# Weights converted in pairs of blocks, q and k in one transfer, and a new planned order in a fused attention and gated-MLP kernel

## The chip, the cores and the metric

The kernel runs on one core of a Trainium2 chip. The metric is the device time of one execution in microseconds (us), less is better. TensorE (PE) does matrix products into PSUM, VectorE (DVE), ScalarE (ACT) and GpSimd (POOL) work on data in SBUF (and, but for POOL, in PSUM), and all transfers are issued by SyncE (SP).

## The reference

Two steps follow each other, in float32, with a batch of 8, 576 positions, 8 heads of 64, a model width of 512 and an inner width of 1,024. The weights come as float64.

```python
scores = scale * np.matmul(q, k.transpose(0, 1, 3, 2))
mask_local = (rel >= 0) & (rel < 32)                          # heads 0..3
mask_strided = (rel >= 0) & (pos[None, :] % 32 == pos[:, None] % 32)   # heads 4..7
attn = softmax(np.where(masks, scores, -1e9))
x = (attn @ v).transpose(0, 2, 1, 3).reshape(B, S, H * D)

h = np.maximum(x @ w_in, 0.0)
conv_out = sum over k of conv_w[k] * h shifted by k - 1 along the positions
gate = 1.0 / (1.0 + np.exp(-conv_out))
out = (h * gate) @ w_out
```

## The kernel before

**Attention** is done by head pairs: four for each batch, 32 in all, in the order 0, 2, 1, 3. Positions of the strided heads are permuted on the host, so that both masks become a band of 64 keys for each block of 32 queries. For one head pair `probabilities` (lines 422 to 463) puts mask and scores in one half of the PSUM bank group `r` (lines 433, 442), takes the maximum (454), subtracts it (455), takes the exponential on ACT (457), sums (458), inverts (460), scales on POOL (461) and transposes on DVE (463). `values` (465 to 521) multiplies with v (482) into both halves of `r`, and then stores the result x as a sum of two operands of the fast matmul format: the high part `xh` is a cast on ACT (518), the low part `xl` is the difference on DVE (519). The scores of the next head pair stand ahead of the values of this one. There are two sets of buffers for q, k and v.

**The weights** arrive as float64 words. For one block of 512 elements a partition, `from_f64` (329 to 343) builds a float32 and a tail from the two words: an absolute value on ACT (333) and five instructions on DVE (334, 336, 338, 340, 342), through the work tiles `wa` and `wt`. `convert` (359 to 396) then makes a high and a low part of the weight, in one of three ways that a letter of `SPLIT_W` picks for each of the sixteen blocks: `a` makes the low part on PE with three products (385, 386, 388) and a cast on ACT (389); `v` does less on PE (392, 393) and adds on DVE (395); `p` and `q` add on POOL (376). Eight blocks hold w_in and eight w_out. Three of the first blocks land in the tile `misc`, which later holds h; the others in two tiles `ws`.

**The MLP** runs over nine groups of 512 positions. `mm1` (541 to 560) is the first layer: for each f of eight, four chunks of the model width, three products each (high by high, low weight by high, high weight by low, line 553). `conv_gate` (562 to 595) does ReLU on ACT (569), carries two columns to the next group on POOL (571, 573), multiplies by the middle tap (579 or 582), adds the other two on DVE (588), takes the sigmoid (591) and the gate product (593), and splits the result into `gh` (405) and `gl` (408). `mm2` (597 to 624) is the second layer, again three products for each f (612), a copy from PSUM (618) and the transfer out (622, 624). `gh` and `gl` have rows of 514 words for each f. PSUM has four banks `m` for both layers and for the conversions.

**The order** of all instructions on all engines comes from a planner (class `Plan`, 61 to 242). Every `op` gives an engine, an estimated duration, a due time `at`, and what it reads and writes; `order` (87 to 164) walks a model of the engines in time and, on each, takes the ready operation with the least due time. The due times are made from the constants at lines 26 to 58. `FIRST` orders the first transfers and conversions. The model of the transfers has the constants `RATE` (a rate), `AHEAD` (how far transfers are issued ahead) and two at lines 148 and 149. While PE waits in the first batch, a few products of zeros (`WARM`, `WARM_SCORES`, `WARM_VALUES`; lines 449 and 491) are put in.

Of the kernel before, what the change touches and what calls it, by code (L numbers as in the profile page):

```python
# [10 lines left out]
F32 = _mybir.dt.float32  # L11
# [10 lines left out]
W = 32  # L22
# [5 lines left out]
AHEAD = 4.0  # L28
ACT_PENALTY = 0
PE_PENALTY = 1  # L30
RATE = 212.0
SWITCH = 0.1

EYE_AT = -56.45
MASK_AT = [-7061.8, -67.27]
CONV_AT = 1385.62
# [4 lines left out]
FIRST_AT = [10013.72, -673.01, -2108.52, 354.38, -675.63]  # L41
CG = [-4502.12, -3977.93, -595.29, 279.54, 48.45, 1488.79, -926.05, -8.92]
AT = [-81.82, -823.34, 1719.98, 17.64, 1599.9, -3890.54, 1345.53, -249.03, 373.38, -2039.0]
GROUP_AT = [330.52, 57.25, -611.52, -158.19, -150.04, -174.24, 1340.78, 429.88, 10027.77]
MM1_STEP = 184.14
MM2_AT = [2846.14, 3562.43, 4063.58, 1041.1, -789.0, 1030.2, 1543.77, -2620.09, 3072.12]
MM2_STEP = 3698.29
ATTENTION_AT = [[1642.69, -1181.42, 70.28, 1735.09], [-58.27, 1008.41, -184.07, -40618.96], [2456.96, 1326.28, -665.66, 1109.36], [-769.08, -2427.12, 1428.65, 831.45], [467.77, 1376.9, 1.5, 781.18], [-13410.3, 547.67, 1062.12, -6885.62], [-5118.76, 1131.26, -697.05, 294.98]]
LOAD_Q = -4714.94
LOAD_V = -1312.32  # L50
W_IN_AT = [1388.4, -1343.86, -1012.12, -1705.32, -1354.59, 160.36, 671.61, -934.52]
W_OUT_AT = [3058.3, -555.74, -1216.5, -322.67, 371.26, -447.54, -1462.81, -8211.41]
SPLIT_W = "vaqaavaavvvaavaa"
SPLIT_G = "vvvvvvvv"
FIRST_SPLIT_G = "vvvvvpvp"
MAJOR = 0
FIRST_GATE = "vvpppppv"
FIRST_SCALE = "aaaaaaaa"


class Plan:
# [25 lines left out]
    def order(self, at):  # L87
# [17 lines left out]
        while True:  # L105
# [41 lines left out]
            if e == "dma":  # L147
                moved = max(moved, t + 1.3) + dur * 1024 / RATE / 1000
                free[e] = max(t + 0.6, moved - AHEAD)
# [96 lines left out]
def tile_banded_attention_gated_mlp(ctx, tc, qT, kT, vw, w_in, conv, w_out, masks_in, picks_in, eye_in, out):  # L246
    nc = tc.nc
    B, NHP, _, S = qT.shape
# [16 lines left out]
    def attention_buffers(pool, i):  # L265
        return (pool.tile([P, S], F32, name=f"q{i}"), pool.tile([P, SP], F32, name=f"k{i}"),
# [17 lines left out]
    gh = mlp.tile([P, NF, N + 2], F32R, name="gh")  # L284
    gl = mlp.tile([P, NF, N + 2], F32R, name="gl")
# [11 lines left out]
    NWS, NWA, NWT, NWL = 2, 2, 2, 2  # L297
# [11 lines left out]
    def load_q(n, at):  # L309
        i, b, hp = slot(n), n // NHP, HPS[n % NHP]  # L310
        q = buffers[i][0]
        op(Q, 288, at, lambda: nc.sync.dma_start(out=q, in_=qT[b, hp]), (), [("q", i)])

    def load_k(n, at):
        i, b, hp = slot(n), n // NHP, HPS[n % NHP]
        k = buffers[i][1]
        op(Q, 288, at, lambda: nc.sync.dma_start(out=k[:, W:], in_=kT[b, hp]), (), [("k", i)])
# [6 lines left out]
    def set_up(i):  # L324
        k, t = buffers[i][1], buffers[i][3]
        op(G, 0.12, -10, lambda: nc.gpsimd.memset(k[:, :W], 0.0), (), [("kpad", i)])
        op(G, 0.11, -3, lambda: nc.gpsimd.memset(t[:, :, 64:65], 1e-9), (), [("tcol", i)])

    def from_f64(hi, lo, a, t, tail, at, kw, ka, kt, kl, short):
        n = 0.15 if short else 0.418  # L330
        m = 0.15 if short else 0.69
        af = a.bitcast(F32)
        op(A, 0.2 if short else 0.667, at, lambda: nc.scalar.activation(out=af, in_=hi.bitcast(F32), func=AF.Abs), [kw], [ka])
# [5 lines left out]
                                                            op1=ALU.bitwise_or), [kw, ka], [kt], lock=True)  # L339
        op(V, n, at, lambda: nc.vector.tensor_scalar(out=a, in0=t, scalar1=-0x800000, scalar2=None,  # L340
                                                     op0=ALU.bitwise_and), [kt], [ka], lock=True)
        op(V, m, at, lambda: nc.vector.scalar_tensor_tensor(out=tail, in0=lo.bitcast(U32), scalar=2.0 ** -52, in1=af,
                                                            op0=ALU.mult, op1=ALU.mult), [kw, ka], [kl], lock=True)

    def convert_conv(at):
# [3 lines left out]
        from_f64(cwords[:, :, 1], cwords[:, :, 0], cwa, cwt, af, CONV_AT, ("W", "c"), ("WA", "c"), ("WT", "c"), ("WA", "c"), True)  # L349
# [6 lines left out]
    def four(x):  # L356
        return x.rearrange("p (c n) -> p c n", c=4)

    def convert(hi, lo, src, at, key, dat=None):
        c = nw[0]  # L360
        nw[0] += 1
        j, k = c % NWA, c % NWT
        if key[0] == "wi" and c < 3:
            i, ws = ("in", c), misc[:, 1024 * c:1024 * c + 1024].bitcast(I32).rearrange("p (n w) -> p n w", w=2)
        else:
            i, ws = c % NWS, words[c % NWS]
        op(Q, 466, at if dat is None else dat, lambda: nc.sync.dma_start(out=ws.rearrange("p n w -> p (n w)"), in_=src.bitcast(I32)), (), [("W", i)])
# [374 lines left out]
```

## Time and profile before

| | |
|---|---|
| median of 3 runs | 542.53 us (542.39 to 544.5) |
| profiled execution | 544.5 us, of which its span 542.7 us |
| instructions | 16,406 |
| busy, share of the span | PE 514.3 us (95%), DVE 378.7 (70%), ACT 316.8 (58%), POOL 90.8 (17%) |
| mean granted TensorE clock | 0.978 |
| moved | 50.77 MB, 94 GB/s on average |

The profile shows one execution. The span runs from the first to the last instruction; the execution's own time has 1.8 us around it. Matmuls are pipelined and their records overlap, so "busy" is the time in which at least one is under way. A line such as L612 is a line of the kernel before.

### The profile page before, as it was taken

The numbers are of one execution on the slowest core, as the hardware profiler recorded it, in microseconds if no ns is written. First come the engines' busy times: TensorE is split into PE (matmuls) and PEld (weight loads), VectorE is DVE, ScalarE is ACT, GpSimd is POOL, SyncE is SP. The second block draws the span as 40 slices with busy tenths as digits, with TensorE's granted clock in tenths as the row PEclk, the third lists the DMA queues.
The fourth block names the chain that finished last, engine by engine and source line by source line (L and its number), as shares of the span: only waits on it lengthen the run. The fifth ranks groups of instructions, "written<-read, shape, count | busy, mean of one in ns | idle before, by whom it ended". The sixth has DMA issues, their size and how long they took to land.

```text
span 542.7 us, 16406 instructions
## 1 busy us (share of the span) xinstructions
PE 514.3 (95%) x7174; PEld 409.5 (75%) x7174; DVE 378.7 (70%) x704; ACT 316.8 (58%) x500; POOL 90.8 (17%) x180
## 2 busy tenths in 40 slices
PE   4667996999999999999999999999999999999997
PEld 3455684677877787788778877887788778888897
DVE  2988889867868577757864977577857874751860
ACT  1345675444866486557756876576648655543751
POOL 1132121232211211121011202211112111100100
PEclk9987699999999999999999999999999999999999
DMA  8745423155034502440233223402350102002001
GB/s 284 235 155 167 139 78 117 39 160 186 1 105 120 181 1 74 119 151 30 74 119 108 75 75 109 162 31 76 118 181 0 33 1 79 0 2 77 1 13 65
DMA packets 22247, 50.77 MB, mean 94 GB/s; under 512 B 2720, under 2 KB 3872, under 8 KB 22176
## 3 DMA queue, kind: packets, MB, share of 16 engines
q1 hardware_dynamic: 22176, 49.73, 28.2%
q8 instruction: 56, 0.92, 0.7%
q14 instruction: 15, 0.12, 0.1%
HBM read 40.28 MB, written 9.44 MB: 92 GB/s over the span
## 4 chain that ended last, share of the span: by engine, by line
PE 89%; DVE 6%; DMA 2%; ACT 1%; issue 1%; SPq 1%; POOL 0%; DVEq 0%; ACTq 0%
PE m L612 37%; PE m L553 37%; PE r L482 6%; PE r L442 4%; PE r L433 1%; PE m L385 1%; DVE misc L588 1%; DMA ws<-in_dram 1%; DVE t L455 1%; DMA q<-in_dram 1%; DVE mx L454 1%; PE r L449 1%; DVE wt L338 0%; DVE wa L336 0%; DVE xl L519 0%
## 5 line engine op out<-in xcount | busy, mean ns | idle before, releaser
L588 DVE SCALAR_TENSOR_TENSOR misc<-misc,cw 128x512 f32<-128x512 f32 (+29 forms) x256 | 121.9, 516 | 40.9 <-ACT misc L579 40.7
L612 PE MATMUL m<-gh,woh 128*128 128x512 f32 (+2 forms) x320 | 124.6, 389 | 2.4 <-ACT misc L569 2.4
L612 PE MATMUL m<-gh,wol 128*128 128x512 f32 (+2 forms) x320 | 119.9, 375 | 0.0
L612 PE MATMUL m<-gl,woh 128*128 128x512 f32 (+2 forms) x320 | 119.7, 374 | 0.0
L553 PE MATMUL m<-xh,wih 128*128 128x512 f32 x288 | 114.2, 397 | 0.7 <-ACT wil L389 0.7
L553 PE MATMUL m<-xl,wih 128*128 128x512 f32 x288 | 113.2, 393 | 0.1
L553 PE MATMUL m<-xh,wil 128*128 128x512 f32 x288 | 113.0, 392 | 0.0
L569 ACT ACTIVATE misc<-m 128x512 f32<-128x512 f32 x72 | 43.1, 598 | 56.8 <-PE m L553 49.5
L612 PEld LDWEIGHTS m<-gh,woh 128*128 128x128 f32 x320 | 60.4, 189 | 15.5 <-ACT misc L569 2.8
L612 PEld LDWEIGHTS m<-gl,woh 128*128 128x128 f32 x320 | 60.7, 190 | 11.6
L612 PEld LDWEIGHTS m<-gh,wol 128*128 128x128 f32 x320 | 60.6, 189 | 9.4
L461 POOL TENSOR_TENSOR t<-t,sm 128x640 f32<-128x640 f32 x32 | 43.1, 1346 | 141.4 <-DVE sm L460 136.7
L553 PEld LDWEIGHTS m<-xh,wih 128*128 128x128 f32 x288 | 54.6, 190 | 13.3 <-ACT wil L389 1.2
L553 PEld LDWEIGHTS m<-xl,wih 128*128 128x128 f32 x288 | 54.5, 189 | 12.2 <-DVE xl L519 0.5
L553 PEld LDWEIGHTS m<-xh,wil 128*128 128x128 f32 x288 | 54.7, 190 | 11.3
L405 ACT CAST gh<-misc 128x512 fp32r<-128x512 f32 (+1 forms) x72 | 44.3, 615 | 29.2 <-DVE misc L593 28.5
L579 ACT ACTIVATE misc<-misc,cw 128x512 f32<-128x512 f32 (+1 forms) x72 | 52.3, 726 | 9.7 <-DVE gl L408 6.6
L408 DVE TENSOR_TENSOR gl<-misc,gh 128x512 fp32r<-128x512 f32 (+1 forms) x70 | 47.8, 686 | 13.8 <-ACT gh L405 13.3
L591 ACT ACTIVATE misc<-misc 128x512 f32<-128x512 f32 (+1 forms) x72 | 44.9, 629 | 17.2 <-DVE misc L588 16.8
L593 DVE TENSOR_TENSOR misc<-misc 128x512 f32<-128x512 f32 (+1 forms) x67 | 46.3, 691 | 11.7 <-ACT misc L591 11.5
L618 ACT COPY misc<-m 128x512 f32<-128x512 f32 (+2 forms) x40 | 21.7, 545 | 44.4 <-PE m L612 39.9
L454 DVE TENSOR_REDUCE mx<-r 128x10 f32<-128x640 f32 x32 | 26.3, 822 | 30.1 <-PE r L442 30.0
(80 smaller groups left out, 544.0 us busy)
## 6 DMA issues: line engine op xcount, KB each, us to landing
v<-in_dram SPq DMA_DIRECT2D x32, 384.0 KB, 3.4
k<-in_dram SPq DMA_DIRECT2D x32, 288.0 KB, 3.9
q<-in_dram SPq DMA_DIRECT2D x32, 288.0 KB, 3.0
out_dram<-misc SPq DMA_DIRECT2D x28, 256.0 KB, 3.1
ws<-in_dram SPq DMA_DIRECT2D x13, 512.0 KB, 3.6
misc<-in_dram SPq DMA_DIRECT2D x3, 512.0 KB, 6.4
out_dram<-misc SPq DMA_DIRECT2D x4, 255.5 KB, 3.7
out_dram<-misc SPq DMA_DIRECT2D x3, 256.5 KB, 2.3
```

The lines of the kernel that those rows point to most:

```text
L405: op(A, ta, at, lambda: nc.scalar.copy(hi(), src), [skey], [(key, "h")])
L408: lambda: eng.tensor_tensor(out=lo(), in0=src, in1=hi().bitcast(F32), op=ALU.subtract),
L454: op(V, 0.826, at + AT[0], lambda: nc.vector.tensor_reduce(out=mx, in_=p3, axis=AX.X, op=ALU.max), ks, [("mx", i)])
L461: op(G, 1.28, at + AT[5], lambda: nc.gpsimd.tensor_tensor(out=t, in0=t, in1=sm.unsqueeze(2).to_broadcast([P, 2 * NBLK, 64]), op=ALU.mult), ...
L482: nc.tensor.matmul(psV[64 * h:64 * h + 64, o:o + n_], v[W * c:W * c + W, h, j], tt[W * c:W * c + W, 64 * NBLK * h + a:64 * NBLK * h + z], ...
L553: nc.tensor.matmul(ps, a[:, c, fs], x[:, c, N * x0:N * x0 + N], start=(n == 0 and m == 0), stop=(n == NC - 1 and m == 2))
L569: op(A, 0.596, at + CG[2], lambda: nc.scalar.activation(out=h[:, 2:N + 2], in_=ps, func=AF.Relu), [kp], [("h", hi)])
L579: op(A, 0.725, at + CG[3], lambda: nc.scalar.activation(out=c_[:, :n], in_=h[:, 1:n + 1], func=AF.Copy, scale=w1), kh + ["cw"], [kc] + new)
L588: op(V, 0.11 + 0.00117 * (z - a), at + CG[4] + 0.4 * k, lambda k=k, wk=wk, a=a, z=z: nc.vector.scalar_tensor_tensor(out=c_[:, a:z], in0=h[ ...
L591: op(A, 0.63, at + CG[5], lambda: nc.scalar.activation(out=c_[:, :n], in_=c_[:, :n], func=AF.Sigmoid), [kc], [kc], table=1)
L593: op(ge, 0.69 if ge == V else 1.28, at + CG[6], lambda: (nc.vector if ge == V else nc.gpsimd).tensor_tensor(out=c_[:, :n], in0=h[:, 1:n + ...
L612: nc.tensor.matmul(ps, a[:, f, ms], y[:, f, tok], start=(f == 0 and n == 0), stop=(f == NF - 1 and n == 2))
```

## The change

- **Conversions** take two blocks, 1,024 elements a partition, in each instruction of `from_f64`; the two blocks still arrive in two transfers. The float32 is built in place, in the upper words of the transfer's tile, so `wt` is gone, and the readers of it step over every second word. There are eight letters of `SPLIT_W` instead of sixteen. The products on PE and their evictions stay at 512 columns, and the three products of `a` are one operation of the plan. `a` stands for six pairs and `q` for two; `q` now is the short form on PE with the add on DVE. The tail has a tile of its own, `wl`, and no longer borrows columns of `xh` and `xl`.
- **q and k** of a head pair stand side by side in one array, with the 32 zero columns between them, and come in one transfer.
- **First batch.** `LOW` lets PE subtract the high part of x from the sum that still stands in `r`, in eight products of 576 columns in all, and ACT casts the rest. `TURN` lets PE turn and normalise the probabilities of head pair 0, by products with diagonal blocks that DVE makes, and ACT copies them out.
- **Rows** of `gh` and `gl` have 528 words instead of 514.
- **Order.** All constants are new, the first group has due times of its own (`FIRST_CG`, `FIRST_AT_OP`), and some estimated durations and the model of the transfers changed. In the later groups three of eight low parts of g go to POOL (`SPLIT_G`); in the first group two gate products move from POOL to DVE and two scalings from ACT to DVE. Of the products of zeros 28 are left of 50.

```diff
-AHEAD = 4.0
-RATE = 212.0
-FIRST = "k0 q0 v0 v2 v3 k1 q2 w1 q1 w3 w0 w2 c0 k3 k2 q3 v1 w4"
-WARM_SCORES = [2, 16, 2, 2]
-WARM_VALUES = [2, 18, 8, 0]
-SPLIT_W = "vaqaavaavvvaavaa"
-SPLIT_G = "vvvvvvvv"
-FIRST_SPLIT_G = "vvvvvpvp"
-FIRST_GATE = "vvpppppv"
-FIRST_SCALE = "aaaaaaaa"
+AHEAD = 9.0
+RATE = 300.0
+FIRST = "q0 v3 c0 w2 q1 v1 q3 q2 w0 v0 w1 v2"
+WARM_SCORES = [2, 16, 0, 2]
+WARM_VALUES = [0, 4, 2, 2]
+SPLIT_W = "aaqaaaaq"
+SPLIT_G = "vvpvvpvp"
+FIRST_SPLIT_G = "vvvppvvv"
+FIRST_GATE = "vvvvvppp"
+FIRST_SCALE = "vavaaaaa"
+TURN = "pvvvv"
+LOW = "pppp"
...
-        return (pool.tile([P, S], F32, name=f"q{i}"), pool.tile([P, SP], F32, name=f"k{i}"),
+        qk = pool.tile([P, S + SP], F32, name=f"qk{i}")
+        return (qk, qk[:, S:],
...
-    gh = mlp.tile([P, NF, N + 2], F32R, name="gh")
-    gl = mlp.tile([P, NF, N + 2], F32R, name="gl")
+    gh = mlp.tile([P, NF, N + 16], F32R, name="gh")
+    gl = mlp.tile([P, NF, N + 16], F32R, name="gl")
...
-    words = [const.tile([P, 4 * P, 2], I32, name=f"ws{i}") for i in range(NWS)]
-    wa = [const.tile([P, 4 * P], I32, name=f"wa{i}") for i in range(NWA)]
-    wt = [const.tile([P, 4 * P], I32, name=f"wt{i}") for i in range(NWT)]
-    wl = [x[:, :, 5 * P:6 * P] for x in (xh, xl)]
+    words = [const.tile([P, 8 * P, 2], I32, name=f"ws{i}") for i in range(NWS)]
+    wa = [const.tile([P, 8 * P], I32, name=f"wa{i}") for i in range(NWA)]
+    wl = [const.tile([P, 8 * P], F32R, name=f"wl{i}") for i in range(NWL)]
...
+        qk = buffers[i][0]
+        op(Q, 592, at, lambda: nc.sync.dma_start(out=qk, in_=qkT[b, hp]), (), [("qk", i)])
...
+        for b in range(2):
+            op(Q, 466, (at if dat is None else dat) + 0.01 * b, lambda b=b: nc.sync.dma_start(
+                out=ws[:, 512 * b:512 * b + 512].rearrange("p n w -> p (n w)"), in_=src[2 * j + b].bitcast(I32)), (), [("W", i, b)])
+        t, tail = ws[:, :, 1].bitcast(F32), wl[il]
+        from_f64(ws[:, :, 1], ws[:, :, 0], wa[ia], ws[:, :, 1], tail, at, kw, ka, kt, kl, False)
...
+        op(A, 1.05, at, lambda: nc.scalar.copy(pair(wh), parts(t)), [kt] + kw, [(k, "h") for k in keys])
...
+                def whole(ps=ps, b=b):
+                    nc.tensor.matmul(ps, eye, half(t, b), start=True, stop=False)
+                    nc.tensor.matmul(ps, eyer, half(tail, b), start=False, stop=False)
+                    nc.tensor.matmul(ps, negr, block(wh, b), start=False, stop=True)
+                op(A, 0.59, at, lambda ps=ps, b=b: nc.scalar.copy(block(wlo, b), four(ps)), [("M", mi)], [(key, "l")])
...
+        if TURN[min(n, len(TURN) - 1)] == "p":
+            op(V, 0.49, at + offset[5], lambda: nc.vector.tensor_tensor(
+                out=diag, in0=small.unsqueeze(1).to_broadcast([P, 2 * NBLK, W]),
+                in1=sm.unsqueeze(2).to_broadcast([P, 2 * NBLK, W]), op=ALU.mult), [("sm", i), "small"], ["diag"], lock=True)
+            def turned():
+                for u in range(2 * NBLK):
+                    for x in range(2):
+                        for c in range(NSEG):
+                            nc.tensor.matmul(scores_[W * c:W * c + W, 64 * u + W * x:64 * u + W * x + W],
+                                             ta[W * c:W * c + W, u, W * x:W * x + W], diag[W * c:W * c + W, u], ...)
+            op(A, 0.7, at + offset[10], lambda: nc.scalar.copy(tt, scores_), ks, [("tt", i)])
...
+            if b == 0 and LOW[n] == "p":
+                def rest():
...
+                                nc.tensor.matmul(psV[:, p_:p_ + k_], negr, y, start=False, stop=True, skip_group_check=True)
+                op(T, 0.8, at + offset[11], rest, [("xh", hp, x) for x in halves] + ["negr"], ko, table=4)
+                op(A, 0.162 + 0.00083 * (z - a), at + offset[9], lambda lo=lo, src=src: nc.scalar.copy(lo, src), ko, [("xl", hp, x) for x in halves])
+                continue
```

More of the change, by code (lines that the diff above doesn't have):

```diff
@@ new lines, in block, with pair @@
+        def block(x, b):
+            if kind == "wi":
+                return x[:, :, P * (2 * j + b):P * (2 * j + b) + P]
+            return x[:, 4 * b:4 * b + 4, P * j:P * j + P]
+        def pair(x):
+            if kind == "wi":
+                return x[:, :, 2 * P * j:2 * P * j + 2 * P].rearrange("p c (b n) -> p b c n", b=2)
+            return x[:, :, P * j:P * j + P]
+        def parts(x):
+            if kind == "wi":
+                return x.rearrange("p (b c n) -> p b c n", b=2, c=4)
+            return x.rearrange("p (c n) -> p c n", n=P)
@@ new lines, in half, with four @@
+        def half(x, b):
+            return x[:, 512 * b:512 * b + 512]
+        def four(x):
+            return x.rearrange("p (c n) -> p c n", n=P)
+        wh, wlo = (wih, wil) if kind == "wi" else (woh, wol)
+        how = SPLIT_W[c]
+        if how == "v":
+            op(V, 1.22, at, lambda: nc.vector.tensor_tensor(out=t, in0=t, in1=tail.bitcast(F32), op=ALU.add), [kl] + kw, [kt], lock=True)
+        op(A, 1.05, at, lambda: nc.scalar.copy(pair(wh), parts(t)), [kt] + kw, [(k, "h") for k in keys])
@@ new lines, in convert, with less @@
+        if how == "v":
+            op(V, 1.22, at, lambda: nc.vector.tensor_tensor(out=pair(wlo), in0=parts(t), in1=pair(wh).bitcast(F32), op=ALU.subtract),
+               [kt] + kw + [(k, "h") for k in keys], [(k, "l") for k in keys], lock=True)
+            return
+        for b, key in enumerate(keys):
+            mi = state["m"] % NPM
+            state["m"] += 1
+            ps = psM[mi]
+            if how == "a":
+                def whole(ps=ps, b=b):
+                    nc.tensor.matmul(ps, eye, half(t, b), start=True, stop=False)
+                    nc.tensor.matmul(ps, eyer, half(tail, b), start=False, stop=False)
+                    nc.tensor.matmul(ps, negr, block(wh, b), start=False, stop=True)
+                op(T, 1.4, at, whole, [kt, kl, (key, "h"), "eye", "eyer", "negr"] + kw, [("M", mi)], table=4)
+                op(A, 0.59, at, lambda ps=ps, b=b: nc.scalar.copy(block(wlo, b), four(ps)), [("M", mi)], [(key, "l")])
+            else:
+                def less(ps=ps, b=b):
+                    nc.tensor.matmul(ps, eyer, half(tail, b), start=True, stop=False)
+                    nc.tensor.matmul(ps, negr, block(wh, b), start=False, stop=True)
+                op(T, 0.46, at, less, [(key, "h"), kl, "negr", "eyer"], [("M", mi)], table=4)
+                op(V, 0.69, at, lambda ps=ps, b=b: nc.vector.tensor_tensor(out=block(wlo, b), in0=four(half(t, b)), in1=four(ps), op=ALU.add),
+                   [("M", mi), kt] + kw, [(key, "l")])
@@ L615, in mm2 @@
                 i = 2 * m + f // 4
-                state["last"] = op(T, 0.69 if z - a0 == N else 0.36, at + 3 * t, products,
+                state["last"] = op(T, 0.697 if z - a0 == N else 0.36, at + 3 * t, products,
                                    [(("g", f), "h"), (("g", f), "l"), (("wo", i), "h"), (("wo", i), "l")], [("M", mi)], [])
@@ L671, in tile_banded_attention_gated_mlp @@
                     mm1(g, [f], t0 + MM1_STEP * f, early)
-                if early:
-                    convert_w_out(f, W_OUT_AT[f])
+                if early and f % 2:
+                    convert(w_out, W_OUT_AT[f // 2], "wo", f // 2)
             if g + 1 < B:
```

214 lines of the change are left out of this document (102 added, 112 removed).

## The prediction

> **What bounds the kernel now.** I read the busy times first, then the span cut into stages, then the chain of waits. From the page of the profile:
>
> ```profile
> PE 514.3 (95%) x7174; PEld 409.5 (75%) x7174; DVE 378.7 (70%) x704; ACT 316.8 (58%) x500; POOL 90.8 (17%) x180
> ...
> PE 89%; DVE 6%; DMA 2%; ACT 1%; issue 1%; SPq 1%; POOL 0%; DVEq 0%; ACTq 0%
> ```
>
> TensorE (PE) is busy for 95% of the span and carries 89% of the chain that ended last. An average over stages hides where the rest lies, so here is busy time by stage (columns: window, then us and instruction counts of PE, weight loads, DVE, ACT, POOL, then granted clock, DMA share, GB/s). I put the cuts at the first scores, at the first matmul of the first layer (46.14), at the first of the second layer (82.43), and where the gaps end:
>
> ```profile
> 0.00:7.03 7.03, 1.71 (x14) 0.88 (x15) 0.53 (x3) 1.28 (x1) 0.47 (x8) 1.00 0.67 193
> 7.03:20.00 12.97, 8.33 (x256) 6.93 (x256) 8.63 (x16) 4.60 (x8) 1.79 (x3) 1.00 0.77 283
> 20.00:46.14 26.14, 20.00 (x536) 13.66 (x534) 23.87 (x46) 9.52 (x17) 7.07 (x8) 0.81 0.62 202
> 46.14:82.43 36.29, 32.71 (x277) 24.87 (x275) 30.45 (x52) 25.43 (x40) 7.03 (x11) 0.86 0.37 111
> 82.43:107.00 24.57, 19.76 (x66) 12.78 (x65) 21.22 (x39) 12.72 (x23) 3.10 (x3) 0.93 0.28 86
> 107.00:539.60 432.60, 431.80 (x6031) 350.35 (x6030) 294.01 (x552) 262.88 (x414) 71.38 (x149) 1.00 0.24 79
> ```
>
> After 107 us PE idles 0.8 us in 432.6. Nothing that helps DVE, ACT or the queues can shorten that stage; only less PE work or a faster matmul can. Before 107 PE idles 5.32 + 4.64 + 6.14 + 3.58 + 4.81 = 24.5 us, and from 20 to 107 DVE is busy 75.5 of 87.0 us (87%). There DVE converts sixteen blocks of weights and runs the first batch's softmax, and there the clock is below 1.00: 0.19 × 26.14 + 0.14 × 36.29 + 0.07 × 24.57 = 11.8 us, or 9.8 us for the 83% (72.5 of 87.0) in which PE works. Two neighbouring windows show what goes before a slow stretch:
>
> ```profile
> 25.74:29.16 3.42, 1.32 (x16) 1.32 (x16) 3.42 (x7) 1.34 (x3) 0.00 (x0) 1.00 0.57 217
> 29.16:32.57 3.41, 3.41 (x91) 2.46 (x89) 2.34 (x5) 1.12 (x2) 1.64 (x1) 0.50 0.09 17
> ```
>
> PE worked 1.32 of 3.42 us while DVE worked throughout; the next 3.41 us ran at half clock. So a wait for DVE is paid twice. One such stretch costs up to 1.7 us.
>
> **The change, part by part.**
>
> *Conversions on DVE.* DVE's groups by shape up to 122 us (columns: count | busy us, mean ns | idle before):
>
> ```profile
> L338 DVE SCALAR_TENSOR_TENSOR wt<-ws,wa 128x512 int32<-128x512 int32 x13 | 10.7, 822 | 0.5
> L336 DVE TENSOR_SCALAR wa<-wa 128x512 int32<-128x512 int32 x16 | 7.7, 483 | 0.3
> L334 DVE TENSOR_SCALAR wa<-wa 128x512 f32<-128x512 f32 x16 | 7.6, 476 | 0.5 <-ACT wa L333 0.5
> L340 DVE TENSOR_SCALAR wa<-wt 128x512 int32<-128x512 int32 x16 | 6.6, 415 | 0.2
> ...
> L342 DVE SCALAR_TENSOR_TENSOR xl<-ws,wa 128x512 fp32r<-128x512 uint32 x7 | 4.8, 685 | 0.3
> ...
> L519 DVE TENSOR_TENSOR xl<-r,xh 128x576 fp32r<-128x576 f32 x4 | 3.0, 754 | 1.9 <-ACT xh L518 1.9
> L395 DVE TENSOR_TENSOR wol<-wt,m 128x512 fp32r<-128x512 f32 x4 | 2.7, 685 | 3.1 <-PE m L393 3.1
> ...
> L336 DVE TENSOR_SCALAR cwa<-cwa 128x24 int32<-128x24 int32 x1 | 0.2, 177 | 0.0
> ```
>
> Five instructions a block cost 0.822 + 0.483 + 0.476 + 0.415 + 0.685 = 2.88 us, sixteen times 46.1 us. An instruction over 24 elements takes 0.177 us, one over 512 takes 0.415: 0.49 ns an element. Over 1,024 that makes an estimated 0.665 us for the three one-input ones and 2 × 0.685 − 0.177 = 1.19 us for the two others: 4.38 us a pair of blocks, eight times 35.0 us, so −11.1 us. Two things can eat into it. The first means hold waits (0.822 against 0.685, 0.483 and 0.476 against 0.415; 4.3 us in all) that may stay. And line 340 now reads every second word; at 1.19 us it would take 4.2 us back (−6.9). I take −9, between the two. Beside it, in that stage: four L395 instead of six (−1.4); the first batch's four L519 gone (−3.0); two gates come from GpSimd to DVE and two scalings from ACT (2 × 0.685 + 2 × 0.415 = +2.2). The transpose that head pair 0 no longer does on DVE pays for the product that makes its diagonals. Net −11.2 us.
>
> [...]
>
> What this is worth: DVE carries 6% of the chain, 32.6 us, out of the 84.7 us that it works before 107. If the saving is spread like DVE's work, 38% lands: −4.3 us. If DVE is what holds everything there, all of it: −11.2 us. At 87% busy it is nearer the second. I take **−7.5 us**.
>
> *Work added to PE.* The chain of waits, three stretches:
>
> ```profile
> 63.96 0.86 PE m L385 x2
> 64.82 0.23 PE m L386
> 65.05 0.23 PE m L388
> 65.28 8.17 PE m L553 x36
> 73.45 0.23 PE m L392
> 73.68 0.23 PE m L393
> ```
>
> ```profile
> 119.83 1.03 PE r L482 x62
> ```
>
> A block whose low part PE makes whole (letter a) costs 0.86 + 0.23 + 0.23 = 1.32 us at full clock; there are 12 of them instead of 9: +4.0. The short form costs 0.46; four instead of six: −0.9. The operand now steps over every second word, but at 0.86 us for 512 columns the fp32 product streams nearly four times slower than the 0.23 us ones, so I leave it; if it doubled, 12 × 0.86 = 10 us. Head pair 0 is turned and normalised by 80 small fp32 products, like the 84 of L482 (1.03 us): +1.0. The low part of x takes 576 columns a head pair in eight pieces: 0.26 us by columns, 1.03 if it went like L482; with eight short starts I take 0.5, +2.0 for four (1.0 to 4.1). Sum +6.1. The warm-up products, 50 before and 28 after, stand in waits and count nothing. Where PE idles the new work is free; it works 83% of the time from 20 to 107, and 46 to 82 is almost solid, so I take two thirds: **+4.0 us** (0 to +8.2).
>
> [...]
>
> *Clock.* 11.8 us at 1.7 a stretch are seven stretches. With shorter waits for DVE I count two fewer: **−3.4 us** (bounds −9.8, all gone, and +3.4, two more).
>
> *First batch's chain.* x's low part goes from DVE to PE and ACT. The bank r is freed only after it, and the next scores wait for that:
>
> ```profile
> 39.44 0.68 DVE xl L519
> 40.12 0.04 issue
> 40.16 0.45 PE r L433 x2
> ```
>
> And from ACT's groups:
>
> ```profile
> L333 ACT ACTIVATE wa<-ws 128x512 f32<-128x512 f32 x13 | 8.7, 672 | 3.8 <-DMA ws<-in_dram 1.7 <-DVE xl L342 1.6 <-DVE xh L342 0.5
> ...
> L518 ACT CAST xh<-r 128x576 fp32r<-128x576 f32 x4 | 2.6, 640 | 4.2 <-PE r L482 4.2
> ```
>
> 0.5 us on PE and 0.64 on ACT replace 0.754 on DVE: with one more handover some 0.6 us later, four times 2.4 us. Half of them on the path: **+1.2 us** (0 to +2.4).
>
> *Loads.* q and k of a head pair are one transfer of 592 KB; 32 issues go, and none of them bounds after 107. At the front the same bytes stand ahead of the first scores, but the small picks now queue behind q and k, so the 0.45 us mask products no longer run early: **+0.4 us**. v of head pair 0 moves behind a pair of weight blocks and more; by the transfers' sizes 4.5 MB stand up to its end, and 193 × 7.03 + 283 × 12.97 kB = 5.0 MB had moved by 20 us, so it lands near its old use, and I price it at nothing.
>
> *Rows of 528.* The second layer's products, from the longest pieces of the whole chain, against the first layer's:
>
> ```profile
> 183.86 21.81 PE m L553 x96
> ...
> 479.48 15.38 PE m L612 x66
> ```
>
> 21.81/96 = 0.2272 us against 15.38/66 = 0.2330. If rows of 514 words cause the difference, 864 such products gain 0.0058 each: −5.0 us. Nothing ties the gap to the rows: the two layers differ in weights, banks and neighbours too, and within each such run the eight f start at eight offsets. I take **0**, bounds −5.0 and 0.
>
> *After 107.* Three of eight low parts of every later group go to GpSimd. DVE works 294 of 432.6 us there, so neither that nor the new offsets move the end; a stall would show as PE idle beyond 0.8 us.
>
> **Sum:** −7.5 + 4.0 − 3.4 + 1.2 + 0.4 = −5.3 us. The profiled execution took 544.5 us (span 542.7 and 1.8 around it), 2.0 over the median of the runs, 542.53. So 537.4 for a span, 539.2 for its execution, and 537.2 against the median.
>
> **The rivals.**
>
> *Faster matmuls:* the rows do matter and everything else holds: 537.2 − 5.0 = 532.2. For it: the 2.5% pace gap. Against: the layers differ in more than their rows.
>
> *DVE was all of it:* −11.2 + 4.0 − 6.8 (four stretches) + 1.2 + 0.4 = −12.4, so 530.1. For it: 3.42 of 3.42 us of DVE work in the window ahead of the slow stretch. Against: the chain gives DVE 38%.
>
> *Hidden:* the softmax's latency and PE's added work eat the gain, the clock stays: −4.3 + 4.0 + 1.2 + 0.4 = +1.3, so 543.8. For it: each head pair goes through both banks of r in turn.
>
> *Slower, through bank r:* the copy of x's low part queues on ACT behind conversions that now take up to 2 × 0.672 = 1.34 us each; with two ahead a head pair's r is held 0.6 + 2.7 = 3.3 us longer, four times 13.2. Then −7.5 + 4.0 + 13.2 + 0.4 − 3.4 = +6.7, 549.2. It decides from (7.5 + 3.4 − 4.0 − 0.4)/4 = 1.6 us a head pair on. Against: ACT works 9.5 of 26.1 us in that stage, so a queue of two is rare.
>
> **Numbers.** Forecast 0.43 (own range 533 to 540), faster matmuls 0.12, DVE all of it 0.13, hidden 0.15, slower 0.17. About 0.5%, 2.7 us, is what a measurement of this kernel tells from no change. Faster by more: nearly all of the forecast with the two gains, 0.66; within: hidden and the forecast's upper edge, 0.16; slower 0.18. Range 528 to 546: the lower end lies beyond both gains' prices, the upper takes in hidden and half the way to the bank's price.
>
> **What would show it.** Right: DVE's five conversion lines sum to about 36 us, the first matmul of the first layer starts before 44 us and gaps end before 103, stretches at half clock fall to about five, and the pace of the second layer stays 0.233. Wrong: ACT's copy of x's low part waits over 1 us ahead of the next scores; strided conversions near 1.19 us; the second layer at 0.227; or PE idle after 107 beyond 2 us, which would mean that the moved low parts arrive late.

## The result and the profile after

The changed kernel takes 534.83 us (median of four runs, 534.35 to 535.69); the kernel before, run beside it, 543.2 us (542.39 to 544.5). The ratio is 0.9845, with a 95% interval of 0.9818 to 0.9873: 8.4 us less, between 6.9 and 9.9. The forecast was 537.2 us, 2.4 us above the result; it took 5.3 us off, and 8.4 went. The profiled span fell from 542.7 to 532.2 us, by 10.5. Rows come from one execution each: that of the kernel before was the slowest of its four and that of the changed kernel the fastest, so some 2 us of the 10.5 are not the change's; that of the experiment plain, 541.44 us, is among the three slowest of its eight; and plain_f has none here, as its profiled execution took 567.42 us at a granted clock of 0.846 and is left out of its ratio.

The busy times and the chain of waits, from the page of the changed kernel:

```profile
PE 511.5 (96%) x7352; PEld 410.3 (77%) x7352; DVE 362.3 (68%) x639; ACT 319.7 (60%) x492; POOL 118.3 (22%) x197
...
PE 93%; ACT 2%; DVE 2%; DMA 1%; issue 1%; SPq 1%; DVEq 0%; ACTq 0%
```

PE's busy time fell by only 2.8 us (514.3 to 511.5). What is left of the span fell from 28.4 to 20.7 us, so 7.7 of the 10.5 us are idle time of PE that is gone. DVE's share of the chain went from 6% to 2%. Where the idle time went shows in the same windows as before (columns: window, length, then us and instruction counts of PE, weight loads, DVE, ACT, POOL, then granted clock, DMA share, GB/s):

```profile
0.00:7.03 7.03, 1.25 (x6) 0.73 (x6) 0.81 (x4) 1.28 (x1) 0.36 (x6) 1.00 0.71 189
7.03:20.00 12.97, 7.62 (x331) 6.84 (x334) 10.79 (x20) 4.96 (x6) 0.00 (x0) 0.88 1.02 404
20.00:46.14 26.14, 21.21 (x565) 15.25 (x559) 20.76 (x28) 14.44 (x19) 6.48 (x6) 0.89 0.54 184
46.14:82.43 36.29, 35.25 (x278) 25.21 (x260) 30.39 (x41) 22.42 (x32) 4.04 (x6) 0.93 0.37 116
82.43:107.00 24.57, 24.57 (x545) 19.38 (x535) 22.55 (x37) 20.64 (x32) 9.55 (x12) 1.00 0.36 113
107.00:529.00 422.00, 421.59 (x5685) 342.87 (x5683) 277.05 (x512) 255.96 (x404) 97.89 (x168) 1.00 0.24 78
```

Up to 46.14 us PE's idle time did not fall: it idles 5.78 + 5.35 + 4.93 = 16.06 us, against 5.32 + 4.64 + 6.14 = 16.10. From 46.14 to 107 us it idles 1.04 us, against 3.58 + 4.81 = 8.39. The cuts are those of the kernel before; the changed kernel does six products of its first layer from 37.86 us on, and the next from 46.6 us on. The stretch from 46.14 us on is where the weights of the second layer are converted. Here is a part of the chain of the kernel before in it (columns: start us, us, what); among the pieces left out are more of the same kinds:

```profile
85.09 0.68 DVE xl L342
85.77 0.61 DVE gl L408
...
86.47 0.73 ACT misc L579
...
88.72 0.70 DVE wt L338
...
93.78 3.91 PE m L612 x9
97.69 0.23 PE m L392
97.92 0.24 PE m L393
...
98.19 0.69 DVE wol L395
...
102.04 0.70 DVE wt L338
```

Conversions (L338, L342) stand in one line with the gates' work (L408, L579) of the first group, and PE still does conversion products (L392, L393) at 97 us. Before them it waits 0.5 us for DVE's L342, 1.5 us for L338, and 2.4 us, up to 93.78, for ACT's ReLU (L569), which in the chain comes behind gate work of DVE, ACT and GpSimd. The chain of the changed kernel, from 55.78 us on:

```profile
55.78 0.92 PE m L411 x2
56.70 0.23 PE m L412
56.93 0.23 PE m L413
...
58.54 5.46 PE m L607 x24
64.00 0.90 PE m L411 x2
...
80.42 0.23 PE m L419
```

From 54.64 us to the end of this fence the chain has only pieces of PE. The first layer's products (L607) and the conversions (L411 to L413, L418 and L419) alternate, each conversion's words were ready when PE came to it, and PE's last product of this kind ends at 80.7 us. DVE is as busy as before there (30.39 against 30.45 us from 46.14 to 82.43); but PE waits for none of it from 54.64 us on.

The clock recovered too. Each window ahead of a stretch at half clock, and the stretch, for the changed kernel:

```profile
13.53:16.95 3.42, 0.85 (x78) 0.68 (x56) 3.42 (x6) 2.25 (x2) 0.00 (x0) 1.00 1.03 410
16.95:23.77 6.82, 5.84 (x195) 4.09 (x201) 6.79 (x9) 2.01 (x3) 2.17 (x3) 0.50 0.55 221
40.84:44.25 3.41, 2.07 (x92) 1.90 (x88) 3.38 (x6) 2.56 (x4) 0.41 (x1) 1.00 1.00 377
44.25:51.08 6.83, 6.40 (x88) 4.31 (x88) 4.48 (x7) 2.20 (x4) 1.70 (x1) 0.50 0.45 130
```

The stretches of the kernel before, of which the prediction showed the first:

```profile
39.40:46.22 6.82, 6.06 (x169) 4.07 (x168) 6.16 (x13) 2.02 (x4) 1.92 (x2) 0.50 0.67 221
53.05:63.29 10.24, 8.85 (x98) 6.05 (x99) 10.03 (x18) 6.21 (x9) 1.30 (x1) 0.50 0.59 171
94.01:97.42 3.41, 3.41 (x9) 2.63 (x9) 2.33 (x5) 2.03 (x4) 0.14 (x1) 0.50 0.43 127
```

In units of 3.41 us they were seven and are four; PE's busy time at half clock fell from 3.41 + 6.06 + 8.85 + 3.41 = 21.73 us to 12.24, which is worth half the difference, 4.7 us, if all of this work takes twice as long at half clock. L411 does (2.00 against 0.90 us); L482 of the kernel before took 1.60 us for 65 products against 1.03 for 62, so it may be less.

### The profile page after: what moved, and what is told of

Its sections match the earlier page's. It is cut to its first block, busy times and chain, and to the rows that moved or that the text cites. A ratio compares the mean times of both kernels' runs of the same rounds, so it can differ in the third digit from the quotient of the medians.

```text
span 532.2 us, 16633 instructions
## 1 busy us (share of the span) xinstructions
PE 511.5 (96%) x7352; PEld 410.3 (77%) x7352; DVE 362.3 (68%) x639; ACT 319.7 (60%) x492; POOL 118.3 (22%) x197
## 4 chain that ended last, share of the span: by engine, by line
PE 93%; ACT 2%; DVE 2%; DMA 1%; issue 1%; SPq 1%; DVEq 0%; ACTq 0%
PE m L667 40%; PE m L607 37%; PE r L514 6%; PE r L458 4%; PE m L411 2%; PE r L449 1%; DMA misc<-in_dram 1%; PE r L569 1%; PE m L413 0%; PE m L412 0%; ACT xh L549 0%; PE r L486 0%; DVE t L471 0%; DVE mx L470 0%; ACT wa L334 0%
## 5 line engine op out<-in xcount | busy, mean ns | idle before, releaser
L643 DVE SCALAR_TENSOR_TENSOR misc<-misc,cw 128x512 f32<-128x512 f32 (+29 forms) x256 | 127.9, 546 | 35.9 <-ACT misc L634 35.3
L607 PE MATMUL m<-xh,wih 128*128 128x512 f32 x288 | 113.3, 393 | 0.0
L607 PE MATMUL m<-xh,wil 128*128 128x512 f32 x288 | 112.5, 391 | 0.0
L607 PE MATMUL m<-xl,wih 128*128 128x512 f32 x288 | 112.5, 391 | 0.0
L492 POOL TENSOR_TENSOR t<-t,sm 128x640 f32<-128x640 f32 x31 | 45.3, 1462 | 116.6 <-DVE sm L476 84.0
L667 PEld LDWEIGHTS m<-gh,woh 128*128 128x128 f32 x320 | 60.1, 188 | 12.5
L607 PEld LDWEIGHTS m<-xh,wih 128*128 128x128 f32 x288 | 54.1, 188 | 11.8 <-issue 0.2
L607 PEld LDWEIGHTS m<-xl,wih 128*128 128x128 f32 x288 | 54.2, 188 | 11.5
L607 PEld LDWEIGHTS m<-xh,wil 128*128 128x128 f32 x288 | 54.2, 188 | 11.2
L634 ACT ACTIVATE misc<-misc,cw 128x512 f32<-128x512 f32 (+1 forms) x70 | 50.5, 724 | 11.4 <-DVE gl L434 5.3
L648 DVE TENSOR_TENSOR misc<-misc 128x512 f32<-128x512 f32 (+1 forms) x69 | 47.8, 693 | 13.2 <-ACT misc L646 12.9
L626 POOL COPY misc<-carry 128x2 f32<-128x2 f32 x64 | 19.1, 299 | 132.6 <-DVE misc L648 93.2
```

What stands on the lines that cost most here:

```text
L492: op(G, 1.28, at + offset[5], lambda: nc.gpsimd.tensor_tensor(out=t, in0=t, in1=sm.unsqueeze(2).to_broadcast([P, 2 * NBLK, 64]), op=ALU.mu ...
L607: nc.tensor.matmul(ps, a[:, c, fs], x[:, c, N * x0:N * x0 + N], start=(n == 0 and m == 0), stop=(n == NC - 1 and m == 2))
L634: op(A, 0.725, at + cg[3], lambda: nc.scalar.activation(out=c_[:, :n], in_=h[:, 1:n + 1], func=AF.Copy, scale=w1), kh + ["cw"], [kc] + new)
L643: op(V, 0.11 + 0.00117 * (z - a), at + cg[4] + 0.4 * k, lambda k=k, wk=wk, a=a, z=z: nc.vector.scalar_tensor_tensor(out=c_[:, a:z], in0=h[ ...
L648: op(ge, 0.69 if ge == V else 1.28, at + cg[6], lambda: (nc.vector if ge == V else nc.gpsimd).tensor_tensor(out=c_[:, :n], in0=h[:, 1:n + ...
L667: nc.tensor.matmul(ps, a[:, f, ms], y[:, f, tok], start=(f == 0 and n == 0), stop=(f == NF - 1 and n == 2))
```

## The experiments

The theory that I tested first was that of the prediction: longer conversion instructions take work off DVE, and DVE's waits hold PE. The rival was that the new planned order of the work carries the gain, whatever DVE has to do. Ratios are to the kernel before, run on the same chip in the same series; the changed kernel's own is 0.9845 (0.9818 to 0.9873). Where I give a difference with ±, it is one of two ratios, with both intervals taken together.

### Shorter conversions, same order (conv512)

Each conversion instruction of DVE over 1,024 elements becomes two over 512, one after the other, at the same place in the order.

```diff
-nc.vector.tensor_scalar(out=af, in0=af, ...)
+for z in (0, 512):
+    nc.vector.tensor_scalar(out=af[:, z:z + 512], in0=af[:, z:z + 512], ...)
```

> The changed kernel, with each of the five VectorE instructions of a conversion issued as two over 512 elements instead of one over 1,024; the order of all instructions is the same. VectorE gets some 8 us more work (the five lines from 36.9 to about 45 us) in the first 80 us. If the shorter conversions carry the gain (my step, two thirds of the saving land): the span grows by about 5 us and TensorE's gaps from 46 to 107 us come back in part. If the new order carries it: it grows by less than 1.5 us.

535.18 us (534.7 to 537.94), ratio 0.9854 (0.9817 to 0.9891). DVE's line on its page:

```profile
PE 511.9 (96%) x7352; PEld 410.3 (77%) x7352; DVE 366.8 (69%) x679; ACT 319.9 (60%) x492; POOL 115.0 (22%) x197
```

DVE works 4.5 us more (366.8 against 362.3) in 40 more instructions, where some 8 were expected, and the time is the same: 0.0009 of the ratio is 0.5 us, with some 2.5 us of uncertainty. So the half of DVE's saving that comes from the length of the instructions is worth nothing measurable where the order is the new one.

### Rows of 514 again, same order (rows514)

```diff
-    gh = mlp.tile([P, NF, N + 16], F32R, name="gh")
+    gh = mlp.tile([P, NF, N + 2], F32R, name="gh")
```

and `gl` likewise.

> The changed kernel with the rows of gh and gl back at 514 words, all else the same. My step: no difference, second-layer products at 0.232 to 0.233 us as now. If rows of 528 had helped: +5 us and a slower pace.

534.12 us (534.01 to 536.94), ratio 0.9837 (0.9801 to 0.9873): no effect of the longer rows shows (−0.4 ± 2.5 us with the short ones), and the 5 us that they might have brought lie outside. The longest piece of the second layer's products over 512 columns in the chain of the changed kernel is 84 of them in 19.49 us, 0.2320 us each, against 0.2330 before; with rows of 514 it is 19.54 us.

### More work on PE, same order (whole2)

The fp32 product of each block whose low part PE makes whole is issued twice. The second starts the sum anew, so nothing is left out.

```diff
                 def whole(ps=ps, b=b):
+                    nc.tensor.matmul(ps, eye, half(t, b), start=True, stop=True)
                     nc.tensor.matmul(ps, eye, half(t, b), start=True, stop=False)
```

> The changed kernel, with the float32 product of each of the 12 blocks whose low part TensorE makes done twice (the first result is overwritten): 12 x 0.90 = 10.8 us more TensorE work at full clock, in the same order. My step, two thirds of added TensorE work land: +7.2 us. If TensorE is the bound from 54.6 us on, eight or nine of the twelve land fully and those at the front are partly hidden: +8 to +10.8 us. If VectorE still bounds the first 107 us: under +3 us.

544.97 us (ten runs, 543.05 to 547.64), ratio 1.0023 (0.9999 to 1.0047). From its chain of waits:

```profile
53.61 0.90 PE m L411 x2
54.51 0.90 PE m L412 x2
```

Twelve times 0.90 us are 10.8 us. The span grew from 532.2 to 542.4 us, by 10.2; by the ratios it is 9.7 ± 2.0 us. Work added to PE among the conversions lands all but in full in this order; two thirds would have been 7.2 us.

### Four parts undone, planned anew (plain) and in the kept order (plain_f)

Both have the conversions in instructions of 512 elements, x's low part of the first batch and head pair 0's transpose on DVE, and rows of 514. The first lets the planner put the operations in order anew; in the second every operation keeps its place and its dependences, and only what it issues is another instruction.

```diff
 # plain
-TURN = "pvvvv"
-LOW = "pppp"
+TURN = "vvvvv"
+LOW = "vvvv"
```

```diff
 # plain_f, same place in the order
                 def rest():
+                    return
...
-  lambda lo=lo, src=src: nc.scalar.copy(lo, src)
+  lambda hi=hi, lo=lo, src=src: nc.vector.tensor_tensor(
+      out=lo, in0=src, in1=hi.bitcast(F32), op=ALU.subtract)
```

> The changed kernel without four of its parts: VectorE conversions in pieces of 512, x's low part of the first batch on VectorE, head pair 0 transposed on VectorE, rows of 514. It keeps the new constants, the joint transfer of q and k, the conversion in place and the ways of splitting; the planner orders the changed operations anew with the new due times. If the parts carry the gain: 8 us or more slower than the changed kernel, so about the time of the kernel before. If the order carries it: within 3 us of the changed kernel.

> The changed kernel with the same four parts undone as in the version before (VectorE conversions in pieces of 512, x's low part and head pair 0's transpose on VectorE, rows of 514), but with the changed kernel's order kept: each replaced operation stands where the operation stood that it replaces, so the planner decides nothing anew. If the order carries the gain and replanning cost the other version its 4 us: within 2 us of the changed kernel. If the parts carry it: 4 us or more slower, up to the time of the kernel before.

plain: 538.53 us (536.13 to 541.72), ratio 0.9905 (0.9872 to 0.9937). plain_f: 532.7 us (532.51 to 532.88 in the other three executions), ratio 0.9826 (0.9791 to 0.9861). The gaps are back in the one that was planned anew. Its window from 46.14 us on, then that of the changed kernel:

```profile
46.14:110.00 63.86, 58.20 (x831) 42.52 (x831) 55.10 (x98) 41.92 (x61) 18.66 (x18) 0.92 0.36 112
```

```profile
46.14:110.00 63.86, 62.82 (x894) 46.87 (x874) 54.38 (x79) 44.62 (x66) 16.04 (x19) 0.96 0.36 114
```

PE idles 5.66 us there against 1.04, with nearly the same work on DVE (55.10 and 54.38 us). In plain's shorter executions it may be less. Undone without moving anything, the four parts together cost nothing measurable (−1.0 ± 2.4 us). Planned anew, the same kernel is 3.3 ± 2.3 us slower than the changed one, near the 3 us named for the order and far from the 8 named for the parts. The 4.3 ± 2.6 us between plain and plain_f come from the order alone.

### One part undone, planned anew (lowdve) and in the kept order (lowdve_f)

The same pair of runs with x's low part alone: DVE subtracts, PE's eight pieces a head pair are gone.

> The changed kernel with x's low part of the first batch back on VectorE (one subtraction of 576 columns, 0.754 us, instead of eight products, 1.13 us, and a copy on ScalarE, 0.64 us, for each of four head pairs); the planner orders it anew with the same due times. My step priced the move to TensorE and ScalarE as a loss of 1.2 us through bank r: then this is 1 us faster than the changed kernel or the same. If the move carries the gain that the version without four parts lost: 3 us or more slower, with longer gaps of TensorE between 30 and 56 us.

> The changed kernel with x's low part of the first batch on VectorE and the order kept: the subtraction stands where ScalarE's copy stood, the eight products are left out. If the move to TensorE gains by itself: 2 us or more slower. If only the replanning cost the other version its 3 us: within 1 us of the changed kernel, or faster, since TensorE has 4.5 us less to do between 24 and 56 us.

Planned anew 537.94 us, ratio 0.9908 (0.9877 to 0.9939); in the kept order 533.15 us, ratio 0.9832 (0.9798 to 0.9865). The windows of the two, planned anew first:

```profile
46.14:110.00 63.86, 60.71 (x851) 44.19 (x850) 54.20 (x79) 43.99 (x64) 16.06 (x19) 0.94 0.37 114
```

```profile
46.14:110.00 63.86, 63.86 (x934) 47.45 (x934) 57.12 (x84) 45.87 (x67) 17.61 (x19) 0.97 0.39 123
```

In the kept order PE does not idle at all there, with 2.7 us more work on DVE than in the changed kernel. So giving x's low part to PE was worth nothing measurable (undone in the kept order, −0.7 ± 2.3 us). The kernel planned anew lies 3.4 ± 2.2 us over the changed one, as if the move carried a gain; but it lies 4.1 ± 2.5 us over the same operations in the kept order, so its order is what costs. As I read it, the due times are fitted to one set of operations.

### More buffers in the old order (b_ws4)

In the new kernel the words of the weights lie in tiles for two blocks and t in place, so loads have more room. The kernel before, with four tiles for words instead of two:

```diff
-    NWS, NWA, NWT, NWL = 2, 2, 2, 2
+    NWS, NWA, NWT, NWL = 4, 2, 2, 2
```

> The kernel before with four tiles instead of two for incoming words of the weights (4 x 512 elements, as many as the changed kernel's two of 1,024); the planner orders it anew with the same due times. If the last weight blocks came late because a transfer waits for a free tile (buffer theory): transfers now start earlier, TensorE's gaps from 84 to 111 us shrink, 3 to 5 us faster than the kernel before. If the order of the work on VectorE and TensorE is what made them late (order theory): within 1.5 us.

550.54 us, ratio 1.0144 (1.0104 to 1.0183): 7.8 us slower, which neither theory had named. Its window:

```profile
46.14:110.00 63.86, 51.34 (x410) 35.26 (x411) 54.67 (x90) 36.73 (x61) 13.99 (x18) 0.84 0.29 89
```

PE idles 12.5 us there, 4.0 more than before (63.86 − 55.33 = 8.53). The gaps from 84 to 111 us did shrink, as the buffer theory said, from 5.46 to 3.04 us; but from 54.64 to 80.70 us PE now idles 8.85 us against 0.68, at a mean clock of 0.67. From 46 to 112 us it waits 8.3 us for conversions of DVE (4.5 for L342, 3.8 for L338). The order changed together with the room, so this run does not price the room by itself.

### The short form for w_out, planned anew (qout) and in the kept order (qout_f)

```diff
-SPLIT_W = "aaqaaaaq"
+SPLIT_W = "aaqaqqqq"
```

In qout_f the six blocks take the short form (no fp32 product, DVE adds) at their old places. There the additions of one pair read its words after the transfer of later ones has been issued, so those low parts come from overwritten words.

> The changed kernel with three more pairs of w_out blocks in the short form (letters aaqaqqqq instead of aaqaaaaq): six blocks cost TensorE 0.46 instead of 1.37 us, VectorE 0.69 us more and ScalarE 0.59 us less each. If TensorE is the bound from 54.6 us on, as the doubled products showed: 6 x 0.91 = 5.5 us faster than the changed kernel, about 529.5 us. If VectorE's 4.1 us more hold the weights back: no faster, with new gaps between 55 and 85 us.

> The changed kernel with six w_out blocks in the short form on TensorE and the order kept: the addition on VectorE stands where ScalarE's cast stood. If TensorE is the bound from 54.6 us on and the order was what spoiled the replanned version: 5.5 us faster than the changed kernel, about 529.5 us. If VectorE's 4.1 us more delay the weights or the gates: no faster than 535, with gaps between 55 and 90 us.

Planned anew 542.36 us, ratio 0.998 (0.995 to 1.0009); in the kept order 534.9 us, ratio 0.987 (0.9834 to 0.9905). The first lost 7.3 ± 2.2 us by the ratios although PE has 5.5 us less to do (6 × 0.91). The other outcome that was named came, gaps after 55 us: from 54.64 to 80.70 us PE idles 4.12 us in the first and 5.27 in the second, where the changed kernel has none. In the first, the additions (L421) read the words up to 65.57 us, and behind them the chain waits 4.94 us for the next words. In the second, the chain has a wait of 4.37 us for words behind an addition, and more additions among the conversions; PE waits for L343. So by these chains it is not the new plan alone: additions in these places hold up the words' tiles and the conversions. What a version of qout_f with the right words would take is open.

### Filling PE's waits (warm2)

Twenty products of zeros after the second scores and fourteen about the third head pair's low part are to keep the clock up in three waits.

```diff
+            if n == 1:
+                for _ in range(20):
+                    nc.tensor.matmul(psM[3][:, 0:192], warm_[:, :P], warm_[:, :192], start=True, stop=True)
```

> The changed kernel with products of zeros in three of TensorE's waits: 20 behind the second scores (the wait from 14.4 to 17.9 us) and 7 before and after the low part of the third head pair (41.8 to 44.4 us), into banks that are free; the order of all else is the same. If a quiet window costs a stretch at half clock (clock theory): the two stretches (16.95 to 23.77 and 44.25 to 51.08 us, 12.2 us of TensorE's work at half speed) shrink or go, 2 to 5 us faster. If the front is bound by the chain of softmax, not by TensorE's speed: within 1 us.

537.73 us (534.33 to 539.49), ratio 0.9894 (0.9833 to 0.9956), 2.7 ± 3.7 us over the changed kernel: no gain shown. The half-clock stretches moved instead of going (21.13 to 27.95 and 55.26 to 62.09 us; the granted clock is 0.87 from 20 to 46.14 us and 0.91 from 46.14 to 82.43), and its chain has a stall within the turned products of head pair 0:

```profile
18.03 1.60 PE r L489 x100
19.62 3.28 issue
22.90 0.42 PE r L489 x11
```

It says nothing for or against the clock's part in the gain.

### A version that beats both (best)

The changed kernel's order with three pieces of PE's work given back at their places: x's low part of the first batch to DVE, head pair 0's transpose to DVE with its scaling on GpSimd, and the short form for the four blocks of two w_out pairs, whose additions come before the next transfer into their words.

```diff
-                    nc.tensor.matmul(ps, eye, half(t, b), start=True, stop=False)
-                    nc.tensor.matmul(ps, eyer, half(tail, b), start=False, stop=False)
+                    if not short:    # short = c in (4, 6)
+                        nc.tensor.matmul(ps, eye, half(t, b), start=True, stop=False)
+                    nc.tensor.matmul(ps, eyer, half(tail, b), start=short, stop=False)
```

> The changed kernel in its own order with three pieces of TensorE work taken back to the other engines: the low parts of four more w_out blocks (pairs 4 and 6) in the short form with DVE's addition (-4 x 0.91 = -3.6 us of PE work, +4 x 0.69 on DVE), the first batch's low part of x on DVE (-4 x 1.13 = -4.5 on PE, +4 x 0.75 on DVE), head pair 0 turned by DVE and scaled by GpSimd (-1.2 on PE). Nothing is left out of the computation. If only the order carried the gain and PE's work lands in full, the removed 9.3 us come off the 534.8: some 526 at best; the two earlier runs with parts of this (533.15 and 532.7) kept 2 us of 5.7 at most, so I expect 529 to 532. If the short form's additions on DVE open new waits in the fixed order, PE idles over 4 us after 46 us and the time is 535 or more.

531.6 us (six runs, 530.1 to 532.89), ratio 0.9771 (0.9746 to 0.9796), whose interval lies below that of the changed kernel: 4.0 ± 2.0 us faster than it, 12.4 faster than the kernel before, and inside the 529 to 532 expected. Its page and its window:

```profile
PE 503.4 (95%) x7152; PEld 402.5 (76%) x7152; DVE 367.3 (70%) x647; ACT 314.7 (60%) x483; POOL 119.2 (23%) x198
...
PE 87%; DVE 8%; DMA 2%; ACT 1%; issue 1%; SPq 1%; ACTq 0%
```

```profile
46.14:110.00 63.86, 59.51 (x940) 44.95 (x938) 58.75 (x87) 43.86 (x63) 16.20 (x19) 0.99 0.38 122
```

PE works 8.1 us less and the span is 3.8 us shorter (528.4): half of the saving became idle time. In this window PE idles 4.35 us against the changed kernel's 1.04, over the 4 us named for the bad outcome, though the time of 535 did not come with it. DVE, with 58.75 of 63.86 us busy, is again in the chain for 8%; whether less work for it would gain anything here, no run shows.

## Why the prediction was right, and where its steps were wrong

The time, 534.83 us, lies 2.4 us under the forecast and inside its own range. The direction and the stage were right: after 107 us nothing changed (0.41 us of idle time against 0.8), and the gain lies in PE's waits before it. The reason that carried most of the sum was not, so that the number came so near is in part luck: −7.5 us for a saving that shows no worth in the new order, and too little for the work added to PE, were made up for by gains that the sum does not have.

**Conversions on DVE, size right, worth wrong.** Groups of the changed kernel up to 107 us (columns: count | busy us, mean ns | idle before), seven of the eight pairs for the lines that name their words' tile:

```profile
L339 DVE SCALAR_TENSOR_TENSOR ws<-ws,wa 128x1024 int32<-128x1024 int32 x7 | 8.5, 1217 | 0.3
L343 DVE SCALAR_TENSOR_TENSOR wl<-ws,wa 128x1024 fp32r<-128x1024 uint32 x7 | 8.5, 1216 | 0.3
...
L341 DVE TENSOR_SCALAR wa<-ws 128x1024 int32<-128x1024 int32 x7 | 5.8, 829 | 0.1
L335 DVE TENSOR_SCALAR wa<-wa 128x1024 f32<-128x1024 f32 x8 | 5.5, 688 | 5.1 <-ACT wa L334 5.1
L337 DVE TENSOR_SCALAR wa<-wa 128x1024 int32<-128x1024 int32 x8 | 5.5, 686 | 0.1
...
L341 DVE TENSOR_SCALAR wa<-misc 128x1024 int32<-128x1024 int32 x1 | 0.7, 681 | 0.0
```

A pair takes 1.22 + 1.22 + 0.83 + 0.69 + 0.69 = 4.65 us, eight times 37.2: 8.9 us less than 46.1, where I had taken 9. The strided line 341 (340 before) takes 0.68 us in seven of eight cases, not 1.19; one took 1.70, which lifts the mean of its row to 0.829. The failed step is "What this is worth", the −7.5 us: conv512 gives half the saving back for 0.5 ± 2.5 us, plain_f gives back that half and 3 us more of DVE's work and is not slower. Both are in the new order; what longer instructions would have been worth in the old one was not tried. I took the share of DVE's work in the chain, or its busy share, as the measure. From 20 to 107 us DVE was 87% busy before and 85% after (73.7 of 87.0 us), and yet PE idles 14.5 us there in the one and 6.0 in the other. What differs is which of DVE's jobs came first; that this is the cause is my reading of the two chains, which the pairs of runs below support. (The share itself was also read too high: the 6% are of the whole span, and up to 107 us DVE's pieces of the chain sum to 26.4 us, 31% of 84.7 and not 38%.)

**The step that was missing is the order.** The sum has no term for the new due times ahead of 107 us. The chains above show what they did: before, the last conversions of w_out stand between gates up to 105 us, in the changed kernel PE is done with them at 80.7 us and waits for none from 54.64 us on. Loads came earlier too: from 7 to 20 us the queues moved 404 GB/s against 283. The chain of the kernel before has a wait of 6.10 us for words from 20.88 us on; that of the changed kernel has one of 6.58 us, but at the start, from 4.01 us on. plain against plain_f and lowdve against lowdve_f show that the order by itself decides over 4.1 to 4.3 us (± 2.6) with the same work (0.0076 and 0.0079 of the ratio). How much of the 7.7 us of idle time belongs to the due times, and how much to the joint transfer of q and k, the words converted in place and the other distribution of gates, is open: I tried none of these without the order, nor the new due times with the old parts. plain, without the four parts and in an order not fitted to it, still has 0.9905, 5.2 us less than the kernel before; where those come from is not shown.

**Work added to PE, too low twice.** By the chain above a whole block is 0.90 + 0.23 + 0.23 = 1.36 us, twelve 16.3 us instead of nine times 1.32: +4.4, near the +4.0 reckoned, with an operand that steps over every second word at 0.90 against 0.86. x's low part was mis-sized. Three head pairs' pieces in the chain:

```profile
34.63 1.14 PE r L569 x8
...
42.54 1.12 PE r L569 x8
...
54.64 1.14 PE r L569 x8
```

That is 1.12 to 1.14 us, not 0.5, and over my bound of 1.03: +4.5 us for four, not +2.0. With −0.9 and about +1.2 for the turning (2.36 us in the chain, at half clock) the sum is +9.2 instead of +6.1. That two thirds of it land was too low by whole2, where 9.7 ± 2.0 of 10.8 us do; lowdve_f, which takes off the 4.5 us, gains only 0.7 ± 2.3. There PE idles 7.38 us from 20 to 46.14 us against 4.93 in the changed kernel, so part of what was taken off became waiting. The 128-byte step of head pairs 2 and 3 (1.14 us at 34.63 and 54.64 us) costs next to nothing beside the contiguous one of pair 1 (1.12 us at 42.54).

**Clock, right in sign.** Two stretches fewer were forecast, −3.4 us; three went, −4.7. That it followed the waits which the order took away is likely and not shown; warm2 moved the stretches and did not remove them.

**First batch's chain: its price too low, its sign right.** The copy of x's low part stands in the chain ahead of the mask products twice:

```profile
26.66 1.12 ACT wa L334
27.79 0.54 ACT xl L572
...
28.36 0.33 PE r L449 x8
...
43.68 0.65 ACT xl L572
...
44.37 0.47 PE r L449 x6
```

For head pair 1 (at 43.68 us) it waits for nothing on ACT. For head pair 0 it does: PE's eight products end at 26.98 us, ACT is still on a conversion (L334), the copy starts at 27.68, and PE waits 1.38 us for it. That is the mechanism of the rival through bank r, but once, and with a delay of 0.7 us where over 1 us was named as its sign. Up to 60 us PE waited 2.3 us for x's low part before (for L519); it now waits 2.1 us for the copy and 2.6 us for the cast ahead of the new products. That is 2.4 us more, the upper end of the range 0 to +2.4, where +1.2 was taken. Of the 0.6 us a head pair behind that range, 0.39 come from rows (0.5 + 0.64 − 0.754); the rest was my estimate of one more handover, for which the chain has 0.02 us from PE's products to ACT's copy (at 43.66) and 0.04 from the copy to PE (at 44.33). As PE's idle time up to 46.14 us did not grow, other waits shrank.

The signs came. The first layer starts at 37.86 us instead of 46.14, before the 44 that was named, though with six products only; the rest follows from 46.6 us on. The last wait of over half a microsecond ends at 54.64 us, not just before 103, and the stretches at half clock are four, not five.

**Rows and loads.** The rows were priced right, at 0. At the front, up to 20 us, PE idles 11.13 us against 9.96, 1.2 us more where +0.4 was taken; from 20 to 46.14 us it idles 1.2 us less.

The sum by the measured terms, on the span: −7.7 of idle time and −2.8 of PE's busy time, together −10.5 us. In the −2.8 are +9.2 of added work and some −4.7 of half clock; the −7.3 that are left are a remainder and not measured. I can only divide them by reasoning: 22 warm-up products fewer, about 2 us (18 of them take 1.84 us in the chain before), and a shorter start at low clock, about 5 (below).

## What to carry to other kernels

A busy engine in the chain of waits doesn't say that less work for it helps (DVE had 6% of the chain here, and half its saving given back costs 0.5 ± 2.5 us): look which of its jobs the waiting engine needs, and whether they could stand earlier. Before a part of a change is credited with a gain, undo that part with every operation kept in its place; undone through a planner, it is charged with a worse order too (0.9905 against 0.9826 here). And once an order is good, work that is taken off the bounding engine at fixed places, a little at a time, can still pay (0.9771).

## What the runs showed of the hardware

**The record of the clock starts late.** The windows up to the first record (25.74 us before, 13.53 after) show a granted clock of 1.00, yet the same products run slowly there. From the chain of the kernel before, 17.75 us into the span, against the 1.03 us for 62 of them at 119.83 that the prediction quotes:

```profile
17.75 1.61 PE r L482 x65
...
53.77 1.60 PE r L482 x65
```

The second row stands in a stretch recorded at 0.50, and takes the same time. If PE ran at half clock up to the first record, its 15.41 us of work there before and 5.95 us after cost up to 7.7 and 3.0 us more than at full clock. The difference, 4.7 us of the gain, is an estimate that the records don't show.

**Half clock came after short waits.** In the window ahead of the stretch from 44.25 us PE worked 2.07 of 3.41 us, and no single wait in it was over 0.75 us; the next 6.83 us ran at 0.50.

**Eight short products cost more than their columns.** Pieces of 2 and 16 columns took 0.250 and 0.206 us as recorded, those of 126 and 144 columns 0.321 and 0.310; the whole of 288 × 2 columns takes 1.13 us, 0.14 a piece, where 576 columns at the 0.23 us that 512 take in the chain would be an estimated 0.26. Each piece has its own load of the same 128 × 128 weights, and the eight loads at 34.63 us take 0.97 us; whether these or the products set the time is not separated.

**Slow one-input instructions of DVE beside GpSimd.** The one L341 that took 1.70 us instead of 0.68 ran from 22.15 us on, while GpSimd was on L492 from 21.13 to 23.23 us. In the kernel before an L336 took 1.38 us instead of 0.42 from 36.72 us on, while GpSimd was on L408 from 36.54 to 37.81 us. The two coincide; that GpSimd held DVE up was not tested.

**A stall without a releaser.** In warm2 PE stood still for 3.28 us amid equal products with their inputs there (the row above). I don't know its cause; the changed kernel doesn't have it.
